# A cached attention block on one core: wider projection products, K and wq split over two load queues, one store

## The chip, the cores and the metric

The kernel runs on one core of one Trainium2 chip. The metric is the device time of one execution in microseconds; a program on one core has one span, and the time counts from before its first instruction to after its last. The core has five engines that work side by side and wait for each other through semaphores: PE (matrix products, results in PSUM), DVE (vector work and 32x32 block transposes), ACT (activations and copies), POOL (copies and fills) and SP (which only issues transfers here). Transfers from HBM into on-chip memory (SBUF) are issued by SP or ACT, each with a queue of its own, and run on 16 DMA engines that both queues share.

## The reference

Grouped-query attention with a cache: 8 sequences of 4 new tokens, 32 query heads over 8 K/V heads (4 query heads each), 2048 cached positions, heads of 128, all in bfloat16.

```python
B, Sq, D = 8, 4, 512
Hq, Hkv, Sk, Dh = 32, 8, 2048, 128
q = (x @ wq).reshape(B, Sq, Hq, Dh).transpose(0, 2, 1, 3)
k = jnp.repeat(k_cache, rep, axis=1)
v = jnp.repeat(v_cache, rep, axis=1)
scores = jnp.einsum("bhqd,bhkd->bhqk", q, k) * (Dh ** -0.5)
p = softmax(scores, axis=-1)
o = jnp.einsum("bhqk,bhkd->bhqd", p, v)
out = o.transpose(0, 2, 1, 3).reshape(B, Sq, Hq * Dh) @ wo
```

K and V hold 33.5 MB each, wq and wo 4.2 MB each; x and the output are 32 KB each.

## The kernel before

The work is cut into 8 units (`units`): a unit is a half of the K/V heads (4 heads, `gg`) and a pair of sequences (`bp`). K and V of one unit are 4 MB each. A ring in SBUF has 4 slots of 4 MB (`ring`, `NS = 4`), each `[128 partitions, 2, 8192]` elements, where the middle index is the sequence of the pair. `loads` is the order in which the slots are filled: K of unit 0, wq, K of unit 1, V0, K2, V1, K3 and so on, V7, wo. `issue(done)` (L128) issues loads as long as slots are free in the program's count; the queue then waits on semaphores until the slot's last readers are through. Nearly all loads are issued by SP. ACT issues x and wq (L102) ahead of its own work. Each transfer counts on one of eight semaphores, which the framework gives out in turn, and a transfer waits until the last one with the same semaphore has landed.

The program is written out in order (`manual_schedule`); each engine executes its part of it in that order. At the start DVE and POOL fill buffers with zeros, DVE turns the first sequence of K0 (`turn`, L170, 4 transposes per sequence), PE transposes x, and once wq is there 32 products of 512 columns make the queries (L350), in two halves `gg`, each over four rows `r` of wq and four heads. Four products with different `g` write to different groups of 32 partitions. ACT copies the result, DVE transposes it (L361) and POOL places it in `q_bd` (L186).

Then the loop over `u` (L368): DVE turns K of unit `u`, PE makes its scores (L197, 32 products of 512 columns), DVE takes the maxima (L210), ACT the exponentials (L231), DVE transposes them (L245), ACT and POOL spread them (L255), and PE makes the value products of the unit before (L271, 64 products of 256 columns). `scaled` and `joined` (L283, L289) divide by the sums, `by_tokens` (L306) permutes the rows, and `to_rows` (L315) copies and transposes a finished half into `oP`.

The tail (L400 to L409) is the projection by wo. wo lies in the last slot as 32 rows of 512 columns per partition (16 rows for each half). `project` (L325) has two products of 256 columns for each row, one into partitions 0 to 31 of `out_ps` and one into partitions 32 to 63. The first 4 rows come before the last `by_tokens`, the other 28 after it. wo arrives in five pieces (`load_wo`, L112): 16 rows, then 8, 4, 2 and 2. At the end ACT copies `out_ps` to `out_sb`, and ACT and SP store a half of the columns each. After the last instruction of the kernel, SP checks all semaphores two by two and the engines meet at a barrier.

Of the kernel before, what the change touches and what calls it, by code (L numbers as in the profile page):

```python
# [8 lines left out]
BF16 = mybir.dt.bfloat16  # L9
FP32 = mybir.dt.float32  # L10
# [7 lines left out]
def kernel(  # L18
# [9 lines left out]
    nc = tc.nc  # L28

    B, Sq, D = x.shape  # L30
    _, Hkv, Sk, Dh = k_cache.shape
    HqDh = wq.shape[1]
    Hq = HqDh // Dh
    rep = Hq // Hkv
    T = B * Sq
    R = D // 128
# [3 lines left out]
    NG = Hkv // G  # L40
    NB = 2
    NP = B // NB
    NU = NG * NP
# [6 lines left out]
    DH = D // 2  # L50
    RW = 16
# [5 lines left out]
    const = ctx.enter_context(tc.tile_pool(name="const", bufs=1))  # L57
# [5 lines left out]
    psum_e = ctx.enter_context(tc.tile_pool(name="psum_e", bufs=1, space=bass.MemoryType.PSUM))  # L63
# [5 lines left out]
    ring = ring_pool.tile([128, NS, NB, C * Dh], BF16, name="ring")  # L69
    x_sb = const.tile([T, D], BF16, name="x_sb")  # L70
# [6 lines left out]
    q_bd = [const.tile([128, NB, J * 2, G, NB, Q], BF16, name=f"q_bd{i}") for i in range(2)]  # L77
    p_bd = [const.tile([128, CH // 2, G, 32, 2], BF16, name=f"p_bd{i}") for i in range(4)]
    oP = [const.tile([128, RW, T], BF16, name=f"oP{i}") for i in range(NG)]
    out_sb = const.tile([2 * T, DH], BF16, name="out_sb")  # L80

    units = [(gg, bp) for gg in range(NG) for bp in range(NP)]
    slot_of = {}
# [2 lines left out]
    def take(key):  # L86
        slot_of[key] = n_loads[0] % NS
        n_loads[0] += 1
        return slot_of[key]

    def load_kv(kind, u, parts):

        gg, bp = units[u]
        slot = take((kind, u))
        src = (k_cache if kind == "k" else v_cache)[NB * bp : NB * bp + NB, G * gg : G * gg + G]
        rows = src.rearrange("b g (s c) d -> (g s) b (c d)", c=C)
        n = C * Dh
        for b0, b1, h0, h1 in parts:
            h0, h1 = int(h0 * n), int(h1 * n)
            yield nc.sync.dma_start(ring[:, slot, b0:b1, h0:h1], rows[:, b0:b1, h0:h1])  # L100

    def load_wq():  # L102

        slot = take("wq")
        nc.scalar.dma_start(x_sb[:, :], x.flatten_outer_dims())
        rows = wq.rearrange("(p r) n -> p (r n)", r=R)
        to = ring[:, slot, :, :].rearrange("p b n -> p (b n)")
        n = HqDh
        for r0, r1 in ((0, 1), (1, R)):
            nc.scalar.dma_start(to[:, r0 * n : r1 * n], rows[:, r0 * n : r1 * n])  # L110

    def load_wo():  # L112
        slot = take("wo")
        for gg, cuts in ((0, (0, RW)), (1, (0, 8, 12, 14, 16))):
            rows = wo[gg * G * 512 : (gg + 1) * G * 512, :].rearrange("(p r) j -> p (r j)", r=RW)
            for r0, r1 in zip(cuts, cuts[1:]):
                nc.sync.dma_start(ring[:, slot, gg, r0 * D : r1 * D], rows[:, r0 * D : r1 * D])  # L117

    whole = [(0, NB, 0, 1)]
    loads = ["k0", "wq", ("k", 1)]  # L120
    for u in range(NU):
        loads.append(("v", u))
# [5 lines left out]
    def issue(done):  # L128

        while loads and n_loads[0] < done + NS:  # L130
            what = loads.pop()
            if what == "k0":
                for _ in load_kv("k", 0, [(0, 1, 0, 0.5), (0, 1, 0.5, 1), (1, 2, 0, 1)]):
                    pass
            elif what == "wq":
                load_wq()
            elif what == "wo":
                load_wo()
            else:
                last = what == ("v", NU - 1)  # L140
                for _ in load_kv(*what, [(0, NB, 0, 0.5), (0, NB, 0.5, 1)] if last else whole):
                    pass

    issue(0)

    make_identity(nc, ident[:])
# [6 lines left out]
    for r, b in ((r, b) for r in range(rep) for b in range(NB)):  # L153
        nc.gpsimd.tensor_copy(
            out=perm[:, r, 32 - NB * Sq :]
            .rearrange("k (g x) -> k g x", g=G)[:, :, : NB * Sq]
            .rearrange("k g (b s) -> k b g s", b=NB)[:, b],
            in_=by_row[:, r, b],
        )
    for b in range(NB):  # L160
        nc.vector.tensor_reduce(
            out=of_b[:, b : b + 1],
            in_=ident[:, :].rearrange("k (g b q) -> k b g q", g=G, b=NB)[:, b],
# [161 lines left out]
    def project(gg, r0, r1):  # L325
        w = ring[:, slot_of["wo"], gg, :].rearrange("p (r j) -> p r j", r=RW)
        for r in range(r0, r1):
            for half in range(2):
                nc.tensor.matmul(  # L329
                    out_ps[half * T : (half + 1) * T, :],  # L330
                    lhsT=oP[gg][:, r, :],
                    rhs=w[:, r, half * DH : (half + 1) * DH],
                    start=(gg == 0 and r == 0),
                    stop=(gg == NG - 1 and r == RW - 1),
                )

    for t in range(NT):
        turn(0, 0, t)
# [6 lines left out]
    for gg in range(NG):  # L345
        psq = psum_o.tile([128, rep * Dh], FP32, tag="o", name="psq")
        for r in range(R):
            w = ring[:, slot_of["wq"], r // 2, :].rearrange("p (r n) -> p r n", r=2)[:, r % 2, :]
            for g in range(G):
                nc.tensor.matmul(  # L350
                    psq[g * T : (g + 1) * T, :],
                    lhsT=xT_sb[:, r, :],
                    rhs=w[:, (gg * G + g) * rep * Dh : (gg * G + g + 1) * rep * Dh],
                    start=(r == 0),
                    stop=(r == R - 1),
                )
        nc.scalar.copy(  # L357
            out=q_sb[:, gg, :, :, :, :].rearrange("t r j w e -> t (r j w e)"), in_=psq[:, :]
        )
        for i in range(rep):  # L360
            nc.vector.transpose(  # L361
                out=qT[:, gg, :, :, i, :, :].rearrange("w j b s e -> w j b (s e)").bitcast(FP32),
                in_=q_sb[:, gg, i, :, :, :].rearrange("t j w e -> t (j w e)").bitcast(FP32),
            )
    queries(0)

    out_ps = psum_e.tile([2 * T, DH], FP32, tag="e", name="out_ps")
    for u in range(NU + 1):  # L368
        if u < NU:
            for t in range(NT):  # L370
# [19 lines left out]
        if u >= 1:  # L390
# [5 lines left out]
            if u == NU:  # L396
                joined(u - 1)
                by_tokens(u - 2)
        issue(2 + 2 * u)
    project(0, 0, 4)  # L400
    by_tokens(NU - 1)
    to_rows(NG - 1)
    project(0, 4, RW)
    project(1, 0, RW)
    assert not loads
    o2 = out.flatten_outer_dims()
    nc.scalar.copy(out=out_sb[:, :], in_=out_ps[:, :])
    nc.scalar.dma_start(out=o2[:, :DH], in_=out_sb[:T, :])
    nc.sync.dma_start(out=o2[:, DH:], in_=out_sb[T:, :])  # L409


# [28 lines left out]
```

## Time and profile before

| What | Value |
|---|---|
| median of 3 runs | 185.41 us (185.4 to 185.69) |
| the profiled execution's own time | 185.39 us |
| its span | 183.6 us |
| PE busy | 133.2 us (73%) |
| DVE busy | 127.6 us (69%) |
| ACT busy | 73.4 us (40%) |
| POOL busy | 37.8 us (21%) |
| moved by DMA | 75.71 MB, mean 412 GB/s over the span |
| granted TensorE clock, mean | 0.981 |

How to read it: a group line names the line of the kernel, the engine, the operation, the tile written and read, their shapes, how often (x), the busy time and the mean of one. A timeline line gives the start, the time from the first start to the last end, and the same names; what stands in brackets is the idle time ahead of it and what ended that. Products overlap: the next one starts before the one before has ended, so from n products in a row the spacing is (time of the row less the duration of one) divided by n - 1. A windows line gives a stretch, its length, the busy time of PE, weight loads, DVE, ACT and POOL with the number of instructions, then the granted clock, the share of the DMA engines that was busy, and the rate in GB/s. SP's and the queues' own instructions bear a q behind the engine's name.

### The profile page before, as it was taken

The page shows a single profiled execution, that of the slowest core. Times are in us where ns is not written, and L with a number is a line of the kernel's source. Part 1 is how long each engine was busy: PE and PEld are TensorE (multiplying, and loading weights), DVE is VectorE, ACT ScalarE, POOL GpSimd, SP SyncE. Part 2 cuts the span into 40 slices and gives each one's busy share as a digit, 9 for nine tenths or more (in the row PEclk, how much of TensorE's full clock was granted, in tenths as well). Part 3 has the DMA queues.
Part 4 walks back from the last instruction along what each step waited for, and adds up shares of the span by engine and source line. Part 5 has one row for each costly group of instructions (what it writes and reads, how often), then busy time and mean ns, then how long its engine had stood idle before and what let it go on. Part 6 is the DMA issues. An engine that isn't in the chain of part 4 may idle for free.

```text
span 183.6 us, 2325 instructions
## 1 busy us (share of the span) xinstructions
PE 133.2 (73%) x900; PEld 81.1 (44%) x900; DVE 127.6 (69%) x159; ACT 73.4 (40%) x89; POOL 37.8 (21%) x98
## 2 busy tenths in 40 slices
PE   0010069901999699978996899689878978899992
PEld 0000023300358335833682377237623863388871
DVE  6960029168975997499749965997899579859240
ACT  2000020039505940693099009901980298038000
POOL 8700024007000700160034004300520040005000
PEclk9999999995799999999999999999999999999999
DMA  5999999999999999999999999999999999999990
GB/s 177 425 444 437 427 439 432 425 439 421 443 418 443 425 435 427 425 430 428 443 418 443 418 443 427 432 421 432 443 414 450 414 443 425 418 427 441 410 375 23
DMA packets 5947, 75.71 MB, mean 412 GB/s; under 512 B 464, under 2 KB 560, under 8 KB 944
## 3 DMA queue, kind: packets, MB, share of 16 engines
q1 hardware_dynamic: 5552, 71.32, 91.4%
q10 hardware_dynamic: 384, 4.24, 5.5%
q8 instruction: 7, 0.11, 0.2%
q14 instruction: 4, 0.03, 0.0%
HBM read 75.53 MB, written 0.03 MB: 412 GB/s over the span
## 4 chain that ended last, share of the span: by engine, by line
DVE 37%; DMA 27%; PE 18%; ACT 9%; issue 4%; POOL 2%; SPq 1%; ACTq 1%; DVEq 0%; POOLq 0%
DVE kt L174 23%; DMA ring<-in_wo_dram 15%; PE s_ps L197 12%; DMA ring<-in_wq_dram 12%; ACT p_sb L231 8%; DVE stat L210 8%; PE o_ps L271 4%; DVE pt L245 2%; DVE stat L262 2%; PE psq L350 2%; POOL p_bd L255 1%; SPq L117 1%; DVE stat L218 1%; DVE o_sb L289 1%; POOL q_bd L186 1%
## 5 line engine op out<-in xcount | busy, mean ns | idle before, releaser
L197 PE MATMUL s_ps<-kt,q_bd 128*128 128x512 bf16 x256 | 67.0, 392 | 24.4 <-POOL q_bd L186 15.4
L174 DVE STREAM_TRANSPOSE kt<-ring 128x1024 f32<-128x1024 f32 x64 | 73.9, 1207 | 1.4 <-DMA ring<-in_k_cache_dram 1.1
L271 PE MATMUL o_ps<-ring,p_bd 128*128 128x256 bf16 x512 | 57.0, 273 | 0.0
L197 PEld LDWEIGHTS <-q_bd 128*128 128x128 bf16 x256 | 24.6, 98 | 65.9 <-issue 23.0
L271 PEld LDWEIGHTS <-p_bd 128*128 128x128 bf16 x512 | 49.9, 98 | 5.9
L231 ACT ACTIVATE p_sb<-s_ps,stat 128x1024 bf16<-128x1024 f32 x16 | 22.0, 1404 | 71.3 <-DVE stat L218 71.3
L255 ACT COPY p_bd<-pt 32x1024 bf16<-32x1024 bf16 x44 | 45.8, 1040 | 1.4 <-DVE pt L245 0.8
L255 POOL COPY p_bd<-pt 32x1024 bf16<-32x1024 bf16 x16 | 17.0, 1065 | 111.7 <-DVE pt L245 109.2
L210 DVE TENSOR_REDUCE stat<-s_ps 128x1 f32<-128x1024 f32 x16 | 18.8, 1220 | 11.9 <-PE s_ps L197 11.9
L245 DVE STREAM_TRANSPOSE pt<-p_sb 128x512 f32<-128x512 f32 x16 | 11.3, 709 | 16.0 <-ACT p_sb L231 16.0
L186 POOL COPY q_bd<-qT 32x64 bf16<-32x64 bf16 x64 | 13.1, 231 | 19.7 <-DVE qT L361 17.9
L350 PE MATMUL psq<-ring,xT_sb 128*32 128x512 bf16 x32 | 3.8, 626 | 18.0 <-DMA ring<-in_wq_dram 18.0
L361 DVE STREAM_TRANSPOSE qT<-q_sb 128x64 f32<-128x64 f32 x8 | 1.2, 213 | 13.3 <-ACT q_sb L357 13.3
L350 PEld LDWEIGHTS <-xT_sb 128*32 128x32 bf16 x32 | 1.3, 133 | 19.7 <-issue 19.3
L357 ACT CAST q_sb<-psq 128x512 bf16<-128x512 f32 x2 | 1.2, 586 | 20.9 <-PE psq L350 20.9
L148 DVE MEMSET p_bd<- 128x2048 uint32 x3 | 5.3, 1765 | 2.0 <-PEq L424 1.2
L262 DVE TENSOR_SCALAR stat<-of_b,stat 128x2 f32<-128x2 f32 x8 | 5.9, 734 | 0.3
L289 DVE SCALAR_TENSOR_TENSOR o_sb<-o_ps,stat,o_sb 128x128 bf16<-128x128 f32 x8 | 2.5, 315 | 4.7 <-ACT o_sb L283 4.7
L283 ACT ACTIVATE o_sb<-o_ps,stat 128x128 bf16<-128x128 f32 x8 | 2.9, 368 | 5.6 <-PE o_ps L271 5.4
L329 PE MATMUL out_ps<-ring,oP 128*32 128x256 bf16 x64 | 4.4, 274 | 0.3 <-DMA ring<-in_wo_dram 0.2
L341 PE MATMUL xtp<-ident,x_sb 32*128 32x32 bf16 x4 | 0.3, 195 | 4.5 <-DMA x_sb<-in_x_dram 4.5
L329 PEld LDWEIGHTS <-oP 128*32 128x32 bf16 x64 | 3.0, 96 | 1.3 <-issue 0.6
(24 smaller groups left out, 29.8 us busy)
## 6 DMA issues: line engine op xcount, KB each, us to landing
ring<-in_k_cache_dram SPq DMA_DIRECT2D x7, 4096.0 KB, 23.4
ring<-in_v_cache_dram SPq DMA_DIRECT2D x7, 4096.0 KB, 26.3
ring<-in_v_cache_dram SPq DMA_DIRECT2D x2, 2048.0 KB, 26.1
ring<-in_wq_dram ACTq DMA_DIRECT2D x1, 3072.0 KB, 21.7
ring<-in_k_cache_dram SPq DMA_DIRECT2D x2, 1024.0 KB, 7.5
ring<-in_k_cache_dram SPq DMA_DIRECT2D x1, 2048.0 KB, 21.4
ring<-in_wo_dram SPq DMA_DIRECT2D x1, 2048.0 KB, 24.8
ring<-in_wq_dram ACTq DMA_DIRECT2D x1, 1024.0 KB, 10.1
```

Source lines behind the costliest of these rows:

```text
L148: nc.vector.memset(t[:, :, :, :, :], 0.0)
L174: nc.vector.transpose(out=kt[:, :, :, :, :].rearrange("w c j s e -> w (c j s e)").bitcast(FP32), in_=ring[:, slot_of["k", u], b, t * n : ( ...
L186: nc.gpsimd.tensor_copy(out=qb[rows, b, :, g, b, :].rearrange("w (j e) q -> w j e q", e=2), in_=qT[rows, gg, :, NB * bp + b, :, :, :].rear ...
L197: nc.tensor.matmul(s_ps[:, t, :], lhsT=q_bd[u % 2][:, b, 2 * j + e, :, :, :].rearrange("w g b q -> w (g b q)"), rhs=kts[u, b, t][:, :, j, ...
L210: nc.vector.tensor_reduce(out=stats[u][0][:, h : h + 1], in_=s_ps[:, 2 * h : 2 * h + 2, :].rearrange("q t n -> q (t n)"), axis=AX, op=ALU.max,
L231: nc.scalar.activation(out=p_sb[:, :, :, :].rearrange("q c s e -> q c e s"), in_=s_ps[:, 2 * h : 2 * h + 2, :].rearrange("q t (c e s) -> q ...
L245: nc.vector.transpose(out=pt[:, :, :, :].rearrange("s c q e -> s (c q e)").bitcast(FP32), in_=ps[u, h][:, :, :, :].rearrange("q c s e -> q ...
L255: copy(out=pb[rows, :, g, :, :], in_=pt[rows, :, :, :])
L262: nc.vector.tensor_scalar_mul(stats[u][3][:, :], of_b[:, :], stats[u][4][:, :])
L271: nc.tensor.matmul(o_pss[u][:, :, :], lhsT=pbs[u, h][:, i // 2, :, :, i % 2].rearrange("s g q -> s (g q)"), rhs=v[:, :, h * CH + i, :], st ...
L329: nc.tensor.matmul(out_ps[half * T : (half + 1) * T, :], lhsT=oP[gg][:, r, :], rhs=w[:, r, half * DH : (half + 1) * DH], start=(gg == 0 an ...
L350: nc.tensor.matmul(psq[g * T : (g + 1) * T, :], lhsT=xT_sb[:, r, :], rhs=w[:, (gg * G + g) * rep * Dh : (gg * G + g + 1) * rep * Dh], star ...
```

## The change

K of unit 0 was loaded by SP in three pieces. Now its first sequence is loaded by SP and its second by ACT. x is issued by SP behind the first sequence of K0. wq is cut into its first two and last two rows per partition; SP loads the first two, ACT the last two (before, ACT loaded one row and then three). K1, V0 and V1 are loaded as one transfer for each sequence. wo's first half comes in two pieces of 8 rows, and its second half in pieces of 8, 4, 2, 1 and 1 rows. `out_ps` and `out_sb` become `[32, 512]`, and a row of wo takes one product of 512 columns. The result is copied in two halves of the columns, by ACT and by DVE, and stored by SP in one transfer. There are 32 transfers in all instead of 29, and the store, the 32nd, counts on the last of the eight semaphores.

```diff
-    out_sb = const.tile([2 * T, DH], BF16, name="out_sb")
+    out_sb = const.tile([T, D], BF16, name="out_sb")
...
-    def load_kv(kind, u, parts):
+    def load_kv(kind, u, parts, engines=(nc.sync,)):
...
-        for b0, b1, h0, h1 in parts:
+        for i, (b0, b1, h0, h1) in enumerate(parts):
             h0, h1 = int(h0 * n), int(h1 * n)
-            yield nc.sync.dma_start(ring[:, slot, b0:b1, h0:h1], rows[:, b0:b1, h0:h1])
+            engines[i % len(engines)].dma_start(ring[:, slot, b0:b1, h0:h1], rows[:, b0:b1, h0:h1])
 
     def load_wq():
-
         slot = take("wq")
-        nc.scalar.dma_start(x_sb[:, :], x.flatten_outer_dims())
-        rows = wq.rearrange("(p r) n -> p (r n)", r=R)
-        to = ring[:, slot, :, :].rearrange("p b n -> p (b n)")
-        n = HqDh
-        for r0, r1 in ((0, 1), (1, R)):
-            nc.scalar.dma_start(to[:, r0 * n : r1 * n], rows[:, r0 * n : r1 * n])
+        rows = wq.rearrange("(p b r) n -> p b (r n)", b=NB, r=R // NB)
+        for b, engine in enumerate((nc.sync, nc.scalar)):
+            engine.dma_start(ring[:, slot, b, :], rows[:, b])
 
     def load_wo():
         slot = take("wo")
-        for gg, cuts in ((0, (0, RW)), (1, (0, 8, 12, 14, 16))):
+        for gg, cuts in ((0, (0, 8, RW)), (1, (0, 8, 12, 14, 15, RW))):
...
+    by_sequence = [(b, b + 1, 0, 1) for b in range(NB)]
+    by_half = [(0, NB, 0, 0.5), (0, NB, 0.5, 1)]
...
             if what == "k0":
-                for _ in load_kv("k", 0, [(0, 1, 0, 0.5), (0, 1, 0.5, 1), (1, 2, 0, 1)]):
-                    pass
+                load_kv("k", 0, by_sequence, (nc.sync, nc.scalar))
+                nc.sync.dma_start(x_sb[:, :], x.flatten_outer_dims())
...
+            elif what in (("k", 1), ("v", 0), ("v", 1)):
+                load_kv(*what, by_sequence)
             else:
-                last = what == ("v", NU - 1)
-                for _ in load_kv(*what, [(0, NB, 0, 0.5), (0, NB, 0.5, 1)] if last else whole):
-                    pass
+                load_kv(*what, by_half if what == ("v", NU - 1) else whole)
...
         for r in range(r0, r1):
-            for half in range(2):
-                nc.tensor.matmul(
-                    out_ps[half * T : (half + 1) * T, :],
-                    lhsT=oP[gg][:, r, :],
-                    rhs=w[:, r, half * DH : (half + 1) * DH],
-                    start=(gg == 0 and r == 0),
-                    stop=(gg == NG - 1 and r == RW - 1),
-                )
+            nc.tensor.matmul(
+                out_ps[:, :],
+                lhsT=oP[gg][:, r, :],
+                rhs=w[:, r, :],
+                start=(gg == 0 and r == 0),
+                stop=(gg == NG - 1 and r == RW - 1),
+            )
...
-    out_ps = psum_e.tile([2 * T, DH], FP32, tag="e", name="out_ps")
+    out_ps = psum_e.tile([T, D], FP32, tag="e", name="out_ps")
...
-    o2 = out.flatten_outer_dims()
-    nc.scalar.copy(out=out_sb[:, :], in_=out_ps[:, :])
-    nc.scalar.dma_start(out=o2[:, :DH], in_=out_sb[:T, :])
-    nc.sync.dma_start(out=o2[:, DH:], in_=out_sb[T:, :])
+    nc.scalar.copy(out=out_sb[:, :DH], in_=out_ps[:, :DH])
+    nc.vector.tensor_copy(out=out_sb[:, DH:], in_=out_ps[:, DH:])
+    nc.sync.dma_start(out=out.flatten_outer_dims(), in_=out_sb[:, :])
```

## The prediction

> **What bounds the kernel now.** I read the page's slices first, then the chain that ended last, then the tail of the timeline, and last the start. The execution that the profile shows took 185.39 us, of which its span is 183.6 us, so 1.8 us lie around it; the median of the three runs is 185.41. I make the sum against 185.39, which is the median within 0.02.
>
> ```profile
> span 183.6 us, 2325 instructions
> ...
> DMA  5999999999999999999999999999999999999990
> ...
> SPq L100 <- DVE kt L174: 74.1, 8, 19.4
> ...
> 152.16 27.85 DMA ring<-in_wo_dram
> 180.01 0.04 issue
> 180.05 0.41 PE out_ps L329 x4
> 180.46 0.02 issue
> 180.49 0.37 ACT out_sb L407
> ```
>
> The DMA engines are full from 4 us to 180.01, when the last piece of wo lands: the byte stream is one bound. SP waits long for free ring slots (74.1 us for DVE alone), but 8 MB stay queued meanwhile, so no engine starves. But see how little waits for it:
>
> ```profile
> 158.88 2.15 PE L197 MATMUL s_ps<-kt,q_bd 128*128 128x512 bf16 x8 [0.36 <-DVE kt L174]
> 161.09 14.14 PE L271 MATMUL o_ps<-ring,p_bd 128*128 128x256 bf16 x128
> 175.38 0.61 PE L329 MATMUL out_ps<-ring,oP 128*32 128x256 bf16 x8
> 176.12 0.38 PE L306 MATMUL o_pm<-o_sb,perm 128*128 128x128 bf16 x4
> 177.97 1.49 PE L329 MATMUL out_ps<-ring,oP 128*32 128x256 bf16 x24
> 180.05 0.40 PE L329 MATMUL out_ps<-ring,oP 128*32 128x256 bf16 x4 [0.21 <-DMA ring<-in_wo_dram]
> 180.88 0.36 SPq L409 DMA_DIRECT2D out_dram<-out_sb  x1
> ```
>
> PE works almost without a break from 161.09 (the last 128 value products, then 64 projection products) and stands idle before the last four products for 0.21 us only. So a second chain ends nearly together with the bytes: compute that began when wq landed at 23.34, ran through DVE and PE, and left the projection for the last 5 us. Whatever lengthens that chain by more than some tenths of a microsecond lengthens the kernel.
>
> **The change part by part.**
>
> *Projection products of 512 columns.* It removes 64 products of 256 columns (L329) and adds 32 of 512. I ask what a row of wo costs PE. Before: the pair of a row fills partitions 0 to 31 and 32 to 63 of out_ps, two column groups of the array, and the pair runs side by side: 24 products (12 rows) take 1.49, so (1.49 - 0.273) / 11 = 0.111 us per row, which is what one product of 256 columns costs alone (L271: (14.14 - 0.273) / 127 = 0.109). After: one product of 512 columns in one group, with nothing beside it. Its price stands in L197, also 512 columns: the last four of a unit took 1.03 from first start to last end, one lasts 0.377, so (1.03 - 0.377) / 3 = 0.217 per product. I take 0.217. Below it lies 0.111 (if one group could take 512 columns in the time of two groups' 256, for which no row speaks); above it 0.217 + 0.095, if the 32-column weight load were not hidden. L329's loads are hidden now, at a spacing of 0.111, so I keep 0.217.
>
> Placed on the path: the projection starts at 175.38 as before. Rows 0 to 3 take 4 x 0.217 = 0.87, to 176.26 (before they were done in time for the permutation products at 176.12). These move to 176.31, and the remaining 28 rows, which began at 176.43, begin at 176.63. DVE's two transposes into oP come 0.2 later too, at 178.1 for the first, but row 12 of the rest needs them only at 179.23: cover holds. The last row starts at 176.63 + 27 x 0.217 = 182.49; the last product of before started at 180.18. **+2.31 us**, all on the path, for all of wo has landed by then. A product of 512 ends 0.377 after its start, not 0.273: **+0.10**.
>
> The Trainium skill, TensorE: Matmul & The Clock Gate, section Back-to-back issue gap, gives 131 ns as the sustained spacing of products of 512 columns and 216 ns as the isolated one. The trace's 0.217 agrees with the isolated figure, in a stream of loads and products. The mechanism by which the smaller figure would matter is the first rival below.
>
> *Last wo piece one row, wo's first half in two, and three more issues.* The last piece's landing frees one product in place of four (0.41 of chain). That is worth nothing here, since PE reaches the last row 2.5 us after the landing at 180.01. Smaller rows could slow the stream: the last two pieces of 256 KB each took 0.6 us at the full rate, so I bound the price of 1 KB rows at 0 to 0.1, hidden behind PE. The last two issues now wait on SP for V loads of the last unit and the one before it, to land at about 160 and 165; behind them on SP stands only the store, and the queue still holds over 10 us of work. Zero; with the cover gone it would be 0.4 per issue.
>
> *Two copies and one store.* The copy of 64x256 by ACT (0.366) becomes 32x256 by ACT and then 32x256 by DVE. They don't run together: in the built program DVE's copy waits for ACT's semaphore at the value that ACT's copy sets, and the store waits for DVE. DVE takes 0.35 for 128 columns (L289) and 0.69 for 512 (L317); between them 256 columns cost 0.45, plus 0.03 handover: **+0.48** (0.30 to 0.60). The store: ACT's 16 KB landed last, 1.65 after its issue, and SP's 1.45 after its own; SP's alone is left: **-0.20** (-0.20 to +0.10, since it has twice the bytes).
>
> *The last of eight semaphores.* At the end SP checks its semaphores two by two:
>
> ```profile
> L435 SPq EVENT_SEMAPHORE  x4: 28/28/28, 182.6 to 182.8; - x4
> ```
>
> The first of five checks is the one that waits for the stores, and four more at 0.063 follow it. In the built program the store now counts on the eighth DMA semaphore, which is checked last, so the four are done beforehand: **-0.25** (-0.25 to 0, if the order were another).
>
> *First K and wq over both queues.* Bytes first. What must land before queries is k0, x and wq, 8.4 MB, which lie at the head of the two queues before and after, 4.2 MB on each. Before, wq landed at 23.34 and k0's last part at 23.0, so the queues shared evenly then too. I expect both halves of wq at 23.2 (22.7 to 23.6).
>
> ```profile
> its engine sat idle before it (us, times) until:
>   DMA ring<-in_wq_dram: 18.0, 2
> ...
> 23.38 3.18 PE L350 MATMUL psq<-ring,xT_sb 128*32 128x512 bf16 x28 [11.49 <-DMA ring<-in_wq_dram]
> ...
> 27.90:31.39 3.49, 3.49 (x9) 1.25 (x10) 3.33 (x3) 0.00 (x0) 1.75 (x9) 1.00 0.96 413
> 31.39:36.75 5.36, 5.35 (x25) 2.14 (x23) 1.25 (x1) 0.00 (x0) 0.00 (x0) 1.00 1.01 434
> ```
>
> Before, wq's first row came alone, so 4 of the 32 query products were done at 11.3 and 28 remained: 7 groups of four at 0.43. After, the first product needs half of wq, so 8 groups remain: +0.43, less 0.14 for the landing, is 0.3. PE is at half speed there (a product of 512 per 0.43; 25 in 5.36 after 31.39), and if the clock rises at the same 31.39, half of the delay is won back: **+0.15** to where compute starts. A gain is capped: K of unit 7 lands at 150.4 (issued 124.11, 26.3 to landing) and DVE turns it from 150.58, so compute can come forward by 0.2 at most; a loss is not capped. x now lies behind 2 MB of K on SP: 4.4 becomes about 12, and DVE's first four transposes (7.39 and 10.89) run from about 12 to 17. Both hide under the wait for wq until 23.2; without it x would cost 8 us. V0's second half waits on SP for k0's landing at about 12, with 8 MB queued ahead. k1, v0, v1 in halves and the longer queue cost issues of 0.4 on SP, behind full engines: zero.
>
> Sum: 2.31 + 0.10 + 0.48 - 0.20 - 0.25 + 0.15 = +2.6, so 185.39 + 2.59 = **188.0 us**.
>
> **The rivals.**
>
> *A row costs at most 0.134 (not slower).* One mechanism: successive products of 512 overlap. If a row costs 0.134 or less, PE is through at (180.05 - 176.43) / 27 = 0.134, the bytes decide again, the last row starts at 180.06, and copy, store and checks cancel (+0.48 - 0.20 - 0.25): 185.4. For it: before, products of two groups do overlap. Against it: those were two groups; 256 L197 products and 512 L271 products in one group space out by their columns. The Trainium skill, TensorE: Matmul & The Clock Gate, section Back-to-back issue gap, would put the kernel there with its 131 ns. 4 in 100.
>
> *The clock rises later.* The granted clock fell to 0.50 at 41.63 and rose at 48.46, 6.83 apart, and the rise at 31.39 lies 10.24 before the fall: steps of 3.41. If compute's shifted start misses a step, 8 products run at 0.43 in place of 0.217, up to +1.7: 189.0 to 189.7. Against it: before's four times lie within 0.3. The Trainium skill, TensorE: Matmul & The Clock Gate, section What's actually happening, says that the window of 3413 ns runs freely; the steps agree, and that its phase moves no run here shows. 12 in 100.
>
> *The split pays.* wq lands 1 us or more earlier. Then compute gains 0.2, capped by K of unit 7, and the end is 187.6. For: 18.0 us of PE waits for wq. Against: the same 8.4 MB ahead. The Trainium skill, DMA: Bandwidth & Descriptors, section Issuing engines are not separate DMA queues, is against it as well; the shared rate in the first 20 us agrees. 14 in 100.
>
> *Loads of weights not hidden.* 28 x 0.095 more: 190.6. 3 in 100.
>
> **How the numbers follow.** Forecast 67, rivals 4, 12, 14, 3. Its own range is 187.4 to 188.6: -0.6 for a cheaper copy and an earlier wq, +0.6 for a store and checks that gain nothing. The range over the cases goes from 187.1 (the split pays and DVE's copy costs 0.30, with slack) to 189.6 (most of the late clock); outside are the first and the last rival and the edges, some 12 in 100. A change within 0.2% (0.4 us) is about what a measurement can't tell from none: faster 0.02, same 0.03, slower 0.95.
>
> **What would show it.** In the profile after: products of 512 at L326 without a wait for wo, 28 rows at 0.217; the last at about 182.6; DVE's copy starting as ACT's ends; one store; one check of SP's after its landing. The query products begin once, x32, at about 23.2. Wrong would be: rows at 0.13, a wait for wo ahead of the last row, or wq landing before 22.

## The result and the profile after

The changed kernel takes 188.07 us (median of five, 187.71 to 191.84) against 185.41 us before: the ratio is 1.0132, with a 95% interval of 1.0116 to 1.0149. By that ratio it is slower by 2.45 us. One of its five executions took 191.84 us; executions that long (19 of the 73 here with the new start, none of the 27 of the variants below with the old one) are left out of all comparisons, their cause stays open, and the filler's trace below is of one.

The profiled execution took 187.71 us, with a span of 185.8 us; it is the one from which the terms below are read, against 185.39 and 183.6 before. First the tail, from the timeline of the changed kernel (start, length, what, and in brackets the idle time before it and its cause):

```profile
160.86 14.14 PE L269 MATMUL o_ps<-ring,p_bd 128*128 128x256 bf16 x128
...
175.15 1.04 PE L326 MATMUL out_ps<-ring,oP 128*32 128x512 bf16 x4
...
176.12 0.40 PE L304 MATMUL o_pm<-o_sb,perm 128*128 128x128 bf16 x4
...
176.44 6.22 PE L326 MATMUL out_ps<-ring,oP 128*32 128x512 bf16 x28
...
182.70 0.36 ACT L403 CAST out_sb<-out_ps 32x256 bf16<-32x256 f32 x1 [7.25 <-PE out_ps L326]
183.09 0.41 DVE L404 CAST out_sb<-out_ps 32x256 bf16<-32x256 f32 x1 [4.65 <-ACT out_sb L403]
183.53 0.35 SPq L405 DMA_DIRECT2D out_dram<-out_sb  x1
```

The 28 rows run without a break: (6.22 - 0.379) / 27 = 0.216 us each. The group of the projection confirms that nothing holds them up:

```profile
L326 PE MATMUL out_ps<-ring,oP 128*32 128x512 bf16 x32 | 7.3, 380 | 0.0
```

Before, PE stood still for the last piece of wo. Now the last piece of wo has landed at 179.7, and PE is busy until 182.7. The copies follow each other, DVE's beginning as ACT's ends.

The start, and the one place in the middle where the bytes hold compute up:

```profile
22.58 3.17 PE L347 MATMUL psq<-ring,xT_sb 128*32 128x512 bf16 x32 [8.15 <-DMA ring<-in_wq_dram]
```

```profile
150.33 2.37 DVE L172 STREAM_TRANSPOSE kt<-ring 128x1024 f32<-128x1024 f32 x2 [0.62 <-DMA ring<-in_k_cache_dram]
```

All 32 query products start at once, at 22.58 instead of 23.38 for the 28 of before. But at 150.33 DVE waits for K of unit 7, and of the lead that compute then has, 0.2 us is left: the last value products start at 160.86, against 161.09 before.

### The profile page after: what moved, and what is told of

Same layout as the page of the kernel before. It is cut to its first block, busy times and chain, and to the rows that moved or that the text cites. A ratio compares the mean times of both kernels' runs of the same rounds, so it can differ in the third digit from the quotient of the medians.

```text
span 185.8 us, 2266 instructions
## 1 busy us (share of the span) xinstructions
PE 135.6 (73%) x868; PEld 81.3 (44%) x868; DVE 127.9 (69%) x160; ACT 73.4 (39%) x89; POOL 37.6 (20%) x98
## 4 chain that ended last, share of the span: by engine, by line
DVE 35%; DMA 26%; PE 24%; ACT 7%; issue 3%; POOL 2%; SPq 0%; DVEq 0%; ACTq 0%; POOLq 0%
DVE kt L172 23%; DMA ring<-in_k_cache_dram 15%; PE s_ps L195 11%; DMA ring<-in_wq_dram 11%; PE o_ps L269 8%; ACT p_sb L229 7%; DVE stat L208 6%; PE out_ps L326 4%; DVE pt L243 2%; DVE stat L260 2%; POOL q_bd L184 1%; POOL p_bd L253 1%; PE psq L347 1%; DVE o_sb L287 1%; DVE stat L216 1%
## 5 line engine op out<-in xcount | busy, mean ns | idle before, releaser
L347 PE MATMUL psq<-ring,xT_sb 128*32 128x512 bf16 x32 | 3.2, 570 | 8.2 <-DMA ring<-in_wq_dram 8.2
L326 PE MATMUL out_ps<-ring,oP 128*32 128x512 bf16 x32 | 7.3, 380 | 0.0
L354 ACT CAST q_sb<-psq 128x512 bf16<-128x512 f32 x2 | 1.2, 586 | 10.5 <-PE psq L347 10.5
```

The costliest lines, as they stand in the source:

```text
L326: nc.tensor.matmul(out_ps[:, :], lhsT=oP[gg][:, r, :], rhs=w[:, r, :], start=(gg == 0 and r == 0), stop=(gg == NG - 1 and r == RW - 1),)
L347: nc.tensor.matmul(psq[g * T : (g + 1) * T, :], lhsT=xT_sb[:, r, :], rhs=w[:, (gg * G + g) * rep * Dh : (gg * G + g + 1) * rep * Dh], star ...
```

## The experiments

Two theories were kept apart. By the first, the one-group theory, the loss is PE's: a row of wo costs 0.217 us because all of it passes through one group of 32 columns of the array, while before two groups shared it. By the second, the start theory, the loss comes from the new loads at the start. A third, the width theory, agrees with the first on the projection, but blames the 512 columns and not the single group.

**The wide projection alone.** The kernel before, with this edit:

```diff
-    out_ps = psum_e.tile([2 * T, DH], FP32, tag="e", name="out_ps")
+    out_ps = psum_e.tile([T, D], FP32, tag="e", name="out_ps")
...
-            for half in range(2):
-                nc.tensor.matmul(out_ps[half * T : (half + 1) * T, :], ..., rhs=w[:, r, half * DH : (half + 1) * DH], ...)
+            nc.tensor.matmul(out_ps[:, :], ..., rhs=w[:, r, :], ...)
...
-    nc.scalar.dma_start(out=o2[:, :DH], in_=out_sb[:T, :])
-    nc.sync.dma_start(out=o2[:, DH:], in_=out_sb[T:, :])
+    nc.scalar.dma_start(out=o2[:, :DH], in_=out_sb[:, :DH])
+    nc.sync.dma_start(out=o2[:, DH:], in_=out_sb[:, DH:])
```

> The kernel before with the wide projection alone: a row of wo is one product of 512 columns, out_ps is 32x512, ACT copies it in one piece, and the two stores stay. One-group theory (a row costs 0.217 because it passes through one column group): the last product starts 2.3 us later than 180.18, lasts 0.10 longer, and ACT's copy of 512 columns takes about 0.59 in place of 0.37, so +2.6: 188.0 us. Start theory (the loss comes from K0, wq and x on two queues): nothing changes here, 185.4.

Measured: 188.33 us (188.02 to 188.98), ratio 1.0159 (1.0138 to 1.0180). From its timeline:

```profile
175.35 1.04 PE L328 MATMUL out_ps<-ring,oP 128*32 128x512 bf16 x4
...
176.65 6.22 PE L328 MATMUL out_ps<-ring,oP 128*32 128x512 bf16 x28
...
182.90 0.57 ACT L406 CAST out_sb<-out_ps 32x512 bf16<-32x512 f32 x1 [7.25 <-PE out_ps L328]
```

The projection begins where it began before (175.35 against 175.38), and the same 28 rows in 6.22 us put ACT's copy at 182.90 in place of 180.49. This one part makes the whole loss (2.9 us, 188.33 against 185.47 for the kernel before beside it, where the whole change loses 2.45); all loads are as before here.

**The loads of the start alone.** The kernel before, with this edit:

```diff
-                for _ in load_kv("k", 0, [(0, 1, 0, 0.5), (0, 1, 0.5, 1), (1, 2, 0, 1)]):
-                    pass
+                load_kv("k", 0, by_sequence, (nc.sync, nc.scalar))
+                nc.sync.dma_start(x_sb[:, :], x.flatten_outer_dims())
...
-        for r0, r1 in ((0, 1), (1, R)):
-            nc.scalar.dma_start(to[:, r0 * n : r1 * n], rows[:, r0 * n : r1 * n])
+        for b, engine in enumerate((nc.sync, nc.scalar)):
+            engine.dma_start(ring[:, slot, b, :], rows[:, b])
...
+            elif what in (("k", 1), ("v", 0), ("v", 1)):
+                load_kv(*what, by_sequence)
```

> The kernel before with the loads of the start alone (K0 and wq over both queues, x behind K0 on SP, K1, V0 and V1 by sequence); projection, wo and both stores as before. One-group theory: the bytes still decide at 180.0, whatever compute does earlier, so no change but for the end: the two stores come to stand on the sixth and seventh semaphore, two checks of 0.063 less behind them, 185.25 (185.1 to 185.5). Start theory: slower by 2 us or more, 187.5 to 188. If an earlier wq were worth its 0.8 us: 184.6.

Measured: 185.03 to 185.23 us, ratio 0.9981 (0.9970 to 0.9992). The start theory falls: the new loads make nothing slower here, and are faster by 0.2%. About 0.1 us of that would belong to the end, where the stores now stand on the sixth and seventh semaphore and two checks of 0.063 fewer follow them.

**The projection undone.** The changed kernel with two products of 256 columns per row:

```diff
-            nc.tensor.matmul(out_ps[:, :], ..., rhs=w[:, r, :], ...)
+            for half in range(2):
+                nc.tensor.matmul(out_ps[half * T : (half + 1) * T, :], ..., rhs=w[:, r, half * DH : (half + 1) * DH], ...)
...
-    nc.scalar.copy(out=out_sb[:, :DH], in_=out_ps[:, :DH])
-    nc.vector.tensor_copy(out=out_sb[:, DH:], in_=out_ps[:, DH:])
+    nc.scalar.copy(out=out_sb[:, :DH], in_=out_ps[:T, :])
+    nc.vector.tensor_copy(out=out_sb[:, DH:], in_=out_ps[T:, :])
```

> The changed kernel with the projection undone: two products of 256 columns per row again, into two groups of partitions; ACT copies the first group, DVE the second (it waits for ACT), one store on the eighth semaphore, the loads as changed. One-group theory: PE is done before wo has landed, the last row (one pair) starts at 180.05, copies 0.36 + 0.03 + 0.41, store 1.48, one check: 185.25, a little under the kernel before. Start theory: 187.7 or more.

Measured: 185.03 to 185.31 us, ratio 0.9980 (0.9971 to 0.9990); the profiled execution took 185.24. Timeline:

```profile
175.46 0.61 PE L327 MATMUL out_ps<-ring,oP 128*32 128x256 bf16 x8
...
180.30 0.36 ACT L404 CAST out_sb<-out_ps 32x256 bf16<-32x256 f32 x1 [4.54 <-PE out_ps L327]
```

The projection starts later than in the changed kernel (175.46), and yet the copy starts at 180.30, 2.4 us earlier.

**512 columns, but in two groups.** Even rows go to partitions 0 to 31 and odd rows to 32 to 63, with products as wide as in the changed kernel; the odd sum is rounded to bfloat16 before the two are added.

```diff
+            half = r % 2
             nc.tensor.matmul(
-                out_ps[:, :],
+                out_ps[half * T : (half + 1) * T, :],
                 lhsT=oP[gg][:, r, :],
                 rhs=w[:, r, :],
...
-    nc.scalar.copy(out=out_sb[:, :DH], in_=out_ps[:, :DH])
-    nc.vector.tensor_copy(out=out_sb[:, DH:], in_=out_ps[:, DH:])
+    nc.scalar.copy(out=odd, in_=out_ps[T:, :])
+    nc.vector.tensor_tensor(out=out_sb[:, :], in0=out_ps[:T, :], in1=odd, op=ALU.add)
```

> The changed kernel with products of 512 columns as they are, but even rows into partitions 0 to 31 and odd rows into 32 to 63; ACT copies the odd sum to SBUF (rounded to bfloat16 there) and DVE adds the even one. One-group theory: two rows run side by side, 0.11 per row, PE is done before wo has landed, the bytes decide at 180.0 and the longer copy and add (0.59 + 0.70) are paid: 185.9 (185.6 to 186.3). Width theory (a product of 512 columns costs 0.217 of PE in whatever group): as slow as the changed kernel or slower by the add, 188.0 to 188.6.

Measured: 185.56 to 185.89 us, ratio 1.0013 (1.0003 to 1.0023), though copy and add are longer:

```profile
175.26 0.61 PE L327 MATMUL out_ps<-ring,oP 128*32 128x512 bf16 x4
...
180.30 0.58 ACT L405 CAST q_sb<-out_ps 32x512 bf16<-32x512 f32 x1 [4.74 <-PE out_ps L327]
180.91 0.68 DVE L406 TENSOR_TENSOR out_sb<-out_ps,q_sb 32x512 bf16<-32x512 f32 x1 [2.60 <-ACT q_sb L405]
```

Four products of 512 columns take 0.61 us in two groups and 1.04 in one: two pairs spaced by about 0.22 against four products spaced by 0.216. The width theory falls; what counts here is how many groups work at the same time.

One rival remains: that neighbouring rows wait for each other because they are added into the same place in PSUM, which the two groups also changed. The four permutation products of the changed kernel speak against it:

```profile
160.64 0.39 PE L304 MATMUL o_pm<-o_sb,perm 128*128 128x128 bf16 x4
L304 PE MATMUL o_pm<-o_sb,perm x32: 216/218/229, 70.9 to 176.3; 128*128 128x128 bf16 x32
```

They write into four different places of `o_pm` on the same partitions, and their spacing is still (0.39 - 0.218) / 3 = 0.057 us for 128 columns, or 0.45 ns per column, against 0.216 us for 512, or 0.42 ns. So products in the same groups are spaced by their columns where neighbours don't add into one place either.

**One copy in place of two.** The changed kernel, with ACT copying all 32x512.

```diff
-    nc.scalar.copy(out=out_sb[:, :DH], in_=out_ps[:, :DH])
-    nc.vector.tensor_copy(out=out_sb[:, DH:], in_=out_ps[:, DH:])
+    nc.scalar.copy(out=out_sb[:, :], in_=out_ps[:, :])
```

> The changed kernel with one copy of 32x512 by ACT in place of ACT's and then DVE's 32x256. One-group theory with the copies in series: from the start of the last product to the issue of the store 1.25 us become about 1.03 (copy 0.59 in place of 0.36 + 0.03 + 0.41), so 0.2 less than the changed kernel: 187.5 to 188.0. If a copy of twice the columns took twice the time: no change.

Measured: 187.75 and 187.95 us; against the kernel before 1.0128 (1.0108 to 1.0149).

```profile
182.95 0.57 ACT L403 CAST out_sb<-out_ps 32x512 bf16<-32x512 f32 x1 [7.25 <-PE out_ps L326]
183.55 0.35 SPq L404 DMA_DIRECT2D out_dram<-out_sb  x1
```

From the copy's start to the store 0.60 us pass, against 0.83 (182.70 to 183.53) with two copies: the 0.23 is there. In the times it doesn't show clearly, because the projection began 0.25 later in this execution than in the profiled one of the changed kernel.

**The place of the store's semaphore.** The kernel with the projection undone, with four transfers fewer, so that the store counts on the fourth semaphore.

```diff
-            elif what in (("k", 1), ("v", 0), ("v", 1)):
+            elif what in ():
...
-        for gg, cuts in ((0, (0, 8, RW)), (1, (0, 8, 12, 14, 15, RW))):
+        for gg, cuts in ((0, (0, RW)), (1, (0, 8, 12, 14, 15, RW))):
```

> The kernel of two products per row and one store (changed loads at the start), but K1, V0, V1 and the first half of wo as one transfer each: 28 transfers, so the store counts on the fourth semaphore, which is checked first. If the place of the semaphore is worth four checks of 0.063: 0.25 more than with the eighth, 185.5. If the checks cost nothing behind the store: the same, 185.25.

Measured: 185.42 to 185.55 us, against 185.03 to 185.31 with the eighth. The checks of SP between 182.50 and 182.95, first with the fourth semaphore and then with the eighth, whose store landed at nearly the same instant:

```profile
L432 SPq EVENT_SEMAPHORE  x5: 17/28/28, 182.6 to 182.8; - x5
```

```profile
L432 SPq EVENT_SEMAPHORE  x2: 17/22/28, 182.6 to 182.9; - x2
```

In the first all five checks come after the landing. In the second one check is left, and the other of the two belongs to the barrier, which SP reaches in the same window. The medians differ by 0.22; four checks of 0.063 are 0.25. The store was issued at 181.05 and at 181.14, so the four transfers fewer did not delay it.

**The old start with the projection undone.** An edit of the kernel with the projection undone: K0, x and wq as before, and V1 in one transfer.

```diff
-                load_kv("k", 0, by_sequence, (nc.sync, nc.scalar))
-                nc.sync.dma_start(x_sb[:, :], x.flatten_outer_dims())
+                load_kv("k", 0, [(0, 1, 0, 0.5), (0, 1, 0.5, 1), (1, 2, 0, 1)])
...
-        for b, engine in enumerate((nc.sync, nc.scalar)):
-            engine.dma_start(ring[:, slot, b, :], rows[:, b])
+        for r0, r1 in ((0, 1), (1, R)):
+            nc.scalar.dma_start(to[:, r0 * n : r1 * n], rows[:, r0 * n : r1 * n])
```

> The kernel of two products per row and one store on the eighth semaphore, but K0, x and wq loaded as before (K0 by SP in three pieces, x and wq by ACT, V1 whole). One-group theory with the bytes as the other bound: the same time within 0.1, 185.25, since the bytes end at 180.0 either way. If the new start is worth something where PE doesn't decide: 0.2 to 1 us slower than with the new start.

Measured: 185.56 us (185.28 to 185.94), ratio 1.0000 (0.9991 to 1.0008). With the new start the same kernel took 185.23. So where the bytes decide, the new start is worth 0.3 us; the first case expected, no change within 0.1, did not come. In the two traces the last piece of wo lands at 180.26 with the old start and at 179.93 with the new one. The stretches of the two traces from 0 to 4.60 us (the last three numbers are the clock, the busy share of the DMA engines and GB/s), first the old start:

```profile
0.00:4.60 4.60, 0.14 (x4) 0.14 (x4) 2.99 (x2) 1.28 (x1) 4.00 (x9) 1.00 0.59 185
```

```profile
0.00:4.60 4.60, 0.00 (x0) 0.00 (x0) 2.99 (x2) 1.28 (x1) 4.00 (x9) 1.00 0.65 228
```

228 against 185 GB/s in 4.6 us is 0.2 MB, or 0.46 us at 430 GB/s; up to 20 us the old start regains some of it (438 against 430 GB/s over 15.4 us, 0.12 MB), which leaves about 0.2 us of the 0.3.

**A filler that keeps PE awake.** 22 products on constants, whose results are not used, stand ahead of the query products of the changed kernel.

```diff
+    filler = perm[:, :, :].rearrange("k r n -> k (r n)")[:, :512]
+    for i in range(22):
+        nc.tensor.matmul(out_ps[:, :], lhsT=ident[:, :T], rhs=filler, start=True, stop=True)
```

> The changed kernel with 22 products of 512 columns on constants (results not used) between the transposes of x and the query products, so that PE is busy from about 14.5 to 21 or 22.5 us and the clock is up when wq lands. Clock theory (runs of the changed kernel differ because the clock rises in steps of 3.41 us at another phase each time): the query products space by 0.217 per group of four or less, compute starts 1 to 2 us earlier, is held up by the K load of unit 7 (landing 150.3), and every run gives 187.5 to 187.8. If the spread has another cause: runs from 187.7 to 188.2 or more as without the filler.

Measured: 187.69 and 187.86 us. The test is inconclusive, since neither of these two has a trace, and in the trace that was kept the filler didn't do what it was for:

```profile
18.60:25.42 6.82, 4.27 (x38) 1.98 (x40) 0.00 (x0) 0.12 (x1) 0.00 (x0) 1.00 1.00 384
25.43:32.24 6.81, 5.19 (x26) 1.60 (x15) 5.06 (x12) 1.05 (x2) 3.27 (x16) 0.50 1.01 387
```

The clock rose at 18.60 and fell to 0.50 again at 25.43, after PE had stood idle for 2.6 us until wq landed at 24.2.

**The changed kernel again.** The same file.

> The changed kernel once more, beside the one with the filler on the same chip. Clock theory: runs between 187.7 and 188.3, now and then more, with the rise of the clock at another instant in the profile than 25.2. Without it: the rise at the same instant, 25.2, and the same time each run.

Measured: 187.93 to 187.98 us. In its trace the clock rose at 26.9. What the rise is worth is read from four traces together:

| Kernel | clock rises | last score product of unit 0 starts | K of unit 7 lands | last value products start | time of that execution |
|---|---|---|---|---|---|
| changed | 25.18 | 34.29 | 150.31 | 160.86 | 187.71 |
| changed, again | 26.94 | 34.96 | 150.66 | 161.21 | 187.98 |
| changed, one copy | 31.40 | 36.41 | 150.37 | 161.11 | 187.75 |
| projection undone | 26.13 | 34.83 | 150.61 | 161.16 | 185.24 |

The clock does rise at another instant in each execution, and the last score products of unit 0 start up to 2.1 us apart. By unit 7 little of that is left. In three of the four DVE waits there for K (0.62 us in the changed kernel, 1.38 in its second trace); with the rise at 31.40 it comes 0.23 us after K's landing and doesn't wait. The second trace of the changed kernel, then the one with one copy:

```profile
150.68 1.25 DVE L172 STREAM_TRANSPOSE kt<-ring 128x1024 f32<-128x1024 f32 x1 [1.38 <-DMA ring<-in_k_cache_dram]
```

```profile
150.60 1.23 DVE L172 STREAM_TRANSPOSE kt<-ring 128x1024 f32<-128x1024 f32 x1
```

From DVE's first transpose of unit 7 to the last value products it takes 10.5 us in all four. So where DVE waits, K's landing decides when the tail begins, and that landing itself moved by 0.35 us. The rise at 31.40 costs the 0.23 us between K's landing and DVE's start.

**Two versions that keep two groups.** One, shown here as an edit of the kernel with the projection undone, has the new loads (but V1 in one transfer), two products per row, one copy of 64x256 and two stores on the seventh and eighth semaphore. The other is the kernel before, changed only in wo's pieces and in K1's two transfers, which puts its two stores on the same semaphores.

```diff
-    nc.scalar.copy(out=out_sb[:, :DH], in_=out_ps[:T, :])
-    nc.vector.tensor_copy(out=out_sb[:, DH:], in_=out_ps[T:, :])
-    nc.sync.dma_start(out=out.flatten_outer_dims(), in_=out_sb[:, :])
+    nc.scalar.copy(out=out_sb[:, :], in_=out_ps[:, :])
+    nc.scalar.dma_start(out=o2[:, :DH], in_=out_sb[:T, :])
+    nc.sync.dma_start(out=o2[:, DH:], in_=out_sb[T:, :])
```

> The changed loads with two products of 256 columns per row, and the end as before (one copy of 64x256 by ACT, a store by ACT and one by SP), with V1 whole so that the stores count on the seventh and eighth semaphore. Expected: last row at 180.05, copy 0.37, ACT's store 1.65, then the last check: 185.1, the fastest of all by 0.1 to 0.3. If ACT's late store costs more than the copies in series: 185.3 or more.

> The kernel with the changed loads, two products per row and two stores on the seventh and eighth semaphore once more, beside the one with the old start on the same chip. If the new start lets the bytes end earlier: 0.2 to 0.3 less than with the old start, 184.9 to 185.0; if it doesn't: the same.

> The kernel before with its start, its two products per row and its two stores, changed only in wo's pieces (8, 8 and 8, 4, 2, 1, 1 rows) and K1 in two transfers, so that the stores count on the seventh and eighth semaphore. Expected by the terms of the end: one row after the landing (-0.1), two checks of 0.063 behind the late store in place of five (-0.2): 185.2 against 185.5 for the kernel before. If the smaller pieces slow the bytes: 185.5.

Measured: with the new loads 184.87 to 185.08 us, ratio 0.9967 (0.9955 to 0.9980), and in the second run of the same file 184.90 to 185.20, ratio 0.9971 (0.9960 to 0.9982). With the old start 185.29 us (185.06 to 185.45, 12 executions), ratio 0.9985 (0.9976 to 0.9993). Both beat both kernels. The new start is worth 0.2 between them, as expected.

## Why the prediction was right

Forecast 188.0 us (187.1 to 189.6), slower; measured 188.07. By the terms of the sum, in the profiled executions (187.71 less 185.39 is 2.32):

| Term | forecast | measured | from |
|---|---|---|---|
| projection, start of the last product | +2.31 | +2.33 | (182.28 - 175.15) against (180.18 - 175.38) |
| length of the last product | +0.10 | +0.11 | end of PE's work to the copy |
| copies, to the store's issue | +0.48 | +0.44 | 0.83 against 0.39 |
| store to landing | -0.20 | -0.17 | 1.48 against 1.65 |
| checks | -0.25 | -0.25 | 0.09 against 0.33 |
| start of compute, as it reaches the tail | +0.15 | -0.23 | 160.86 against 161.09 |

The measured terms add up to +2.23, as the spans do (185.84 less 183.62); the other 0.1 lies outside the span. Five terms were right. The sixth had the wrong sign, which takes 0.38 off the sum, so the forecast of 188.0 was 0.3 above the profiled execution, and that it falls within 0.1 of the median is partly luck.

*Products of 512 columns.* Right, and for its reason: 0.217 forecast, 0.216 measured, on the path from the first row to the last; e1 has it alone and e5 shows that the second group, not the width, was lost. The delay of 0.2 at the permutation products came too (176.12 when the projection began 0.23 earlier). The figure of 131 ns in the Trainium skill, TensorE: Matmul & The Clock Gate, section Back-to-back issue gap, didn't hold for this stream of loads and products; its isolated 216 ns did.

*wo's pieces.* Right as a zero: wo landed at 179.7 and the last row started at 182.28.

*Copies, store, semaphore.* Right, each within 0.04. DVE's copy waits for ACT's, and e4 shows what the series costs.

*K0 and wq over both queues.* Here the sign was wrong. The step said that wq would land at 23.2 (22.7 to 23.6) and compute start 0.15 later. wq landed at 22.54, and in the traces of the other kernels with the new start at 22.6 to 23.0, the filler's left out. The clock's rise, which the step took to stay at 31.39, came at 25.18. So compute was ahead by 2.1 us at the end of unit 0's scores. What kept that out of the time was the other half of the step, the cap. "Compute can come forward by 0.2 at most", because K of unit 7 lands at 150.4; it came forward by 0.23. The cap isn't fixed, though: in the second trace of the changed kernel K of unit 7 landed at 150.66, and the last value products started 0.12 later than before. Why this landing moves stays open. That the new start moves the bytes' end by 0.3 was priced at zero; in the changed kernel that isn't seen, since its last row starts 2.6 us after the last piece of wo.

*The rivals.* "A row costs at most 0.134" fell with 0.216. "Loads of weights not hidden" fell with the same number. "The split pays" happened in its mechanism and was capped as it said, but its landing 1 us earlier was 0.8 in the profiled execution. "The clock rises later" was right that the rise moves. Its price of up to 1.7 wasn't tested, since no trace that was compared has a rise later than 31.40; of the 2.1 us by which unit 0's scores differ between the rises at 25.18 and 31.40, about 0.2 reached the tail.

## What to carry to other kernels

Look at the output partitions of narrow products before joining them: two products of 256 columns in two groups of 32 partitions cost as much as one of them, and one product of 512 columns in one group costs twice that, whatever it saves in instructions. Where two chains end together, as bytes and PE do here at 180, a change to either can lose in full and gain almost nothing, so ask first what waits at the last common point (here K of the last unit). At the very end, count what stands behind the last product: the second copy in series cost 0.23 us here, and four semaphore checks behind the store cost 0.25.

## What the runs showed of the hardware that was not expected

The clock's first rise moved between 25.2 and 31.4 us from trace to trace, the filler's apart. Within a trace, its rises and falls lie whole steps of 3.41 us apart (in the changed kernel it rose at 25.18, fell at 38.83 and rose at 49.07, which is four and three such steps). The Trainium skill, TensorE: Matmul & The Clock Gate, section What's actually happening, says that the window runs freely, and these traces agree.

The clock also fell where PE had not been idle for a whole step. In the changed kernel it fell to 0.50 at 151.47, and in the step before that PE was busy for 1.30 of 3.40 us:

```profile
148.06:151.46 3.40, 1.30 (x12) 0.92 (x10) 2.71 (x5) 3.35 (x4) 1.31 (x2) 1.00 0.98 419
```

In the thirteen traces other than the filler's, the clock fell after steps in which PE was busy for 43% of the time or less, and stayed up after all steps with 46% or more; one step with 42% left it up, so where the limit lies stays open. The fall at 151.47 lasted to 154.88 and cost next to nothing: from DVE's first transpose of unit 7 to the last value products it took 10.53 us, against 10.51 in the kernel before at the full clock.
